# One fused attention, gated-MLP and channel-mix kernel: the five engine queues put in an order that a table writes out

## The chip, the cores and the metric

The program runs on one core of a Trainium2 chip. A core has five engines with a queue of instructions each: PE (matrix products), DVE (vector), ACT (scalar functions), POOL (a second, slower vector engine) and SP, which here issues every DMA transfer. Each queue runs in its own order; where an instruction needs another engine's result, it waits on a semaphore, and everything behind it in its queue waits with it. The metric is the device time of one launch in microseconds (us), the median of several executions.

## The reference

Three layers run one after the other on float32 data, with B=4 batches, 8 heads, 576 positions and 64 channels a head.

```python
# attention, causal, with a cumulative bias
cum = np.cumsum(np.maximum(s, 0.0), axis=-1)
bias = -(cum[:, :, :, None] - cum[:, :, None, :])
scores = np.where(causal, -1e9, q @ k.T / sqrt(D) + np.minimum(bias, 0.0))
attn = np.exp(scores - max);  attn = attn / (sum + 1e-9);  out = attn @ v
# gated MLP: 512 -> 1024, mixing over positions with w_sg, 512 -> 512
h = gelu(x @ w_in);  u, v = h[..., :512], h[..., 512:]
v_n = (v - mu) / np.sqrt(var + 1e-06) * g_ln
x = x + (u * (einsum('ts,bsd->btd', w_sg, v_n) + b_sg)) @ w_out
# channel mix
xk = mu_k * x + (1 - mu_k) * x_prev;  xr = mu_r * x + (1 - mu_r) * x_prev
y = sigmoid(xr @ w_r) * (np.maximum(xk @ w_k, 0) ** 2 @ w_v)
```

## The kernel before

Every float32 product is made of products of a "hi" part (rounded) and a "lo" part (what the rounding left), three for one. So each operand is split: a cast makes the hi part, and `split_lo` (L70) subtracts it from the original to make the lo part.

**Attention** works by pairs of heads, 16 pairs in all, `attn_pair` (L220). For head number n, a 128-row tile `kq` holds k above q. A cast (L243) puts q's hi part in the lower rows of `QB`, and another (L244) k's hi part in the upper rows of `ka`. Two DMAs (L245, L246) copy these to the other halves, of `qa` and `ka`. Two subtractions by `split_lo` (so their line in the profile is L71) make the lo parts: the lower half of `qa` from `kq` and `QB`, and the lower half of `KB` from `kq` and `ka`. From head 4 on, POOL makes both and the cast to `QB`. Two small DMAs (L234, L235) put rows of the cumulative sum into `QB` and `KB`. The tile numbers count heads: `qa14` is the first head of pair 7. Scores are then two matmuls, L267 (with `ka`, `qa`) and L268 (with `KB`, `QB`), into PSUM tile `sc`; DVE masks them and takes the maximum (L294), ACT takes the exponential (L299), PE transposes (L314, L317, L325, into `tp`, `tq`), ACT or DVE copies the result to SBUF (`pt1`, `pt2`, L319 to L327), and PE multiplies by v (L354, `pv`). In `sc6_1_3`, 6 is the pair, 1 the second head, 3 the block of rows.

`QB`, `KB`, `qa`, `ka` and `kq` have two buffers each, so head 16's `kq` is loaded (L229) into the buffer that head 14's `qa` subtraction read last.

**The gated MLP** of batch b (`moe1`, L399) runs beside the attention of batch b+1: products `v`, `u`, `sg`, `o` all go through `gemm3` (L386). For the first batch its weights `wc` are also made there: `first_wc` (L184) loads half a block of 256 columns as 64-bit words (`wr`, L197), `convert` (L76) turns them to float32 with two ACT operations (L78, L83) and two on DVE (L84, L86) on a tile `wy`, a cast on ACT (L89) and a subtraction on DVE (L71) make `wcs`, and L200 stores them to DRAM. Layer norm of `v` is POOL's (L442 to L444) with the split of the normed `vn` (ACT cast L446, POOL subtraction L71). The approximate gelu is two ACT operations and two on DVE (L552 to L555).

**The channel mix** follows alone: `k` and `r` products (L386), then 7 products in the place of 8 for `k*k @ w_v` (L829).

**What sets the order.** A scheduler that knows a cost for each instruction puts every engine's instructions in order when the program is built. Two things steer it: the sequence in which the code emits work (a generator `a_stream` for attention is advanced beside `moe1` by the rates `RATE` and `LEAD`), and `after(late, early)` (L539), which only forbids `late` to stand ahead of `early`, with no wait of its own.

Of the kernel before, what the change touches and what calls it, by code (L numbers as in the profile page):

```python
# [34 lines left out]
RATE = (1.1, 1, 1, 1)  # L35


@with_exitstack
def fused_kernel(ctx, tc, kqT, vL, s, w_in, g_ln, w_sgT, b_sg, w_out, mu_k, mu_r, w_k, w_v, w_r, out):
    nc = tc.nc  # L40

    const = ctx.enter_context(tc.tile_pool(name="const", bufs=1))
    dram = ctx.enter_context(tc.tile_pool(name="dram", bufs=1, space=bass.MemoryType.DRAM))
# [78 lines left out]
    with tc.high_priority():  # L122
# [7 lines left out]
        for i in range(NSET + 1):  # L130
            eng = nc.gpsimd if i else nc.vector
# [502 lines left out]
    turn, last = [0], [None]  # L634
# [196 lines left out]
    for p in range(TOK // PW):  # L831
# [8 lines left out]
        a = psum2.tile([P, 1 if last_p else 2, 512], F32, tag="ps", name=f"psa_{p}", bufs=4)  # L840
        b, c = (psum2.tile([P, 2, 512], F32, tag="ps", name=f"ps{n}_{p}", bufs=4) for n in "bc")
        if last_p:
            a = (a[:, 0], psum2.tile([P, 1, 512], F32, tag="ps", name=f"psa2_{p}", bufs=4)[:, 0])
# [10 lines left out]
        def block(h, c, ps, r):  # L854

            t = vb.tile([P, 2, HW], F32, tag="t", name=f"t{p}_{h}{c}", bufs=4)
            t0 = p * PW + c * HW
            g = vb.tile([P, 2, HW], F32, tag="gt", name=f"gt{p}_{h}{c}", bufs=3)
            nc.sync.dma_start(out=g, in_=gdram[h][:, :, t0:t0 + HW])
            for i, x in banks(ps):  # L860
                if r is None:
                    nc.vector.scalar_tensor_tensor(out=t[:, i], in0=x, scalar=1.0 / WS, in1=g[:, i], op0=ALU.mult, op1=ALU.mult)
                else:
                    nc.vector.scalar_tensor_tensor(out=t[:, i], in0=x, scalar=1.0 / WS, in1=r[:, i], op0=ALU.mult, op1=ALU.add)
            if r is not None:
                nc.vector.tensor_tensor(out=t, in0=t, in1=g, op=ALU.mult)
            for i in range(2):
                nc.sync.dma_start(out=out[2 * h + i].rearrange("p b s -> p (b s)")[:, t0:t0 + HW], in_=t[:, i])
# [13 lines left out]
        product(a, xs, 4)  # L882
        block(1, 0, a, None)


# [45 lines left out]
```

## Time and profile before

| | |
|---|---|
| median of 3 executions | 648.99 us (648.87 to 653.36) |
| profiled execution | 650.32 us, its span 648.3 us |
| busy: PE / DVE / ACT / POOL | 617.2 / 479.7 / 414.6 / 220.5 us |
| granted clock of PE over the span | 0.997 of full |

The span is the time from the first to the last record of the profiled execution; its own time has 2.0 us more around it. Busy time is the sum over an engine's instructions. In a timeline each row is one instruction or a run of equal ones, with its start and its duration; a bracket gives how long the engine had been idle and what ended the idle time. The granted clock is 1.00 at the full rate of 2.4 GHz and 0.50 at 1.2 GHz.

### The profile page before, as it was taken

The numbers are of one execution on the slowest core, as the hardware profiler recorded it, in microseconds if no ns is written. First come the engines' busy times: TensorE is split into PE (matmuls) and PEld (weight loads), VectorE is DVE, ScalarE is ACT, GpSimd is POOL, SyncE is SP. The second block draws the span as 40 slices with busy tenths as digits, with TensorE's granted clock in tenths as the row PEclk, the third lists the DMA queues.
The fourth block names the chain that finished last, engine by engine and source line by source line (L and its number), as shares of the span: only waits on it lengthen the run. The fifth ranks groups of instructions, "written<-read, shape, count | busy, mean of one in ns | idle before, by whom it ended". The sixth has DMA issues, their size and how long they took to land.

```text
span 648.3 us, 11284 instructions
## 1 busy us (share of the span) xinstructions
PE 617.2 (95%) x3768; PEld 535.7 (83%) x3768; DVE 479.7 (74%) x986; ACT 414.6 (64%) x937; POOL 220.5 (34%) x218
## 2 busy tenths in 40 slices
PE   1879999999999999999999999999999999999997
PEld 1657777878778987888897999888888888999997
DVE  7999788995659844579632878388897869586964
ACT  3889889974658844668641864278766878553530
POOL 7366649688528676267261200000000000000000
PEclk9899999999999999999999999999999999999999
DMA  7776664465553653735314974576764793646543
GB/s 212 186 236 209 162 201 113 154 189 139 182 189 92 176 138 89 234 95 132 110 24 144 316 261 126 144 243 209 244 211 181 233 344 138 198 162 205 208 146 122
DMA packets 68521, 115.08 MB, mean 178 GB/s; under 512 B 19744, under 2 KB 32688, under 8 KB 68464
## 3 DMA queue, kind: packets, MB, share of 16 engines
q1 hardware_dynamic: 68464, 114.37, 56.6%
q8 instruction: 30, 0.49, 0.3%
q14 instruction: 27, 0.22, 0.1%
HBM read 75.63 MB, written 29.20 MB: 162 GB/s over the span
## 4 chain that ended last, share of the span: by engine, by line
PE 80%; DMA 7%; DVE 6%; ACT 4%; issue 2%; SPq 1%; DVEq 0%; ACTq 0%
PE k L386 15%; PE sg L386 8%; PE psa L829 8%; PE r L386 8%; PE o L386 7%; PE v L386 6%; PE u L386 6%; PE pv L354 5%; PE psb L829 4%; PE tp L317 4%; PE sc L267 3%; PE sc L268 3%; PE psc L829 2%; ACT st L299 1%; DMA wsr<-in_w_sgT_dram 1%
## 5 line engine op out<-in xcount | busy, mean ns | idle before, releaser
L386 PE MATMUL k<-x,wk 128*128 128x512 f32 (+1 forms) x480 | 98.9, 368 | 0.0
L386 PEld LDWEIGHTS k<-x,wk 128*128 128x128 f32 x480 | 83.6, 189 | 14.9
L299 ACT ACTIVATE st<-st,mx 128x384 f32<-128x384 f32 (+4 forms) x128 | 75.1, 588 | 17.5 <-DVE mx L294 16.1
L267 PE MATMUL sc<-ka,qa 128*128 128x512 f32 (+3 forms) x180 | 61.1, 356 | 20.2 <-DMA ka<-ka 15.1
L294 DVE CUSTOM_DVE_ANT_0 st<-sc,mask 128x512 f32<-128x512 f32 (+3 forms) x128 | 62.5, 501 | 14.2 <-PE sc L268 11.1
L386 PE MATMUL sg<-wsg,vn 128*128 128x288 f32 x448 | 63.6, 297 | 0.3 <-DVE ga L485 0.3
L386 PEld LDWEIGHTS sg<-wsg,vn 128*128 128x128 f32 x448 | 60.4, 188 | 1.4 <-DVE ga L485 0.6
L268 PE MATMUL sc<-KB,QB 128*128 128x512 f32 (+3 forms) x180 | 56.3, 333 | 0.0
L267 PEld LDWEIGHTS sc<-ka,qa 128*128 128x128 f32 x180 | 33.1, 186 | 26.8 <-issue 18.7
L317 PE MATMUL tp<-ident,st 128*128 128x128 f32 x316 | 50.8, 279 | 0.6 <-ACT st L299 0.3
L354 PE MATMUL pv<-pt,vf 128*64 128x320 f32 (+4 forms) x448 | 50.6, 364 | 0.0
L386 PE MATMUL r<-x,wr 128*128 128x512 f32 (+1 forms) x240 | 49.5, 368 | 0.0
L386 PE MATMUL v<-wv,xs 128*128 128x512 f32 x192 | 48.4, 397 | 0.0
L386 PEld LDWEIGHTS r<-x,wr 128*128 128x128 f32 x240 | 41.9, 189 | 7.5
L648 ACT ACTIVATE yx<-yt,mu 128x64 f32<-128x64 f32 (+4 forms) x64 | 30.4, 529 | 26.5 <-DMA yt<-ydram 25.4
L354 PEld LDWEIGHTS pv<-pt,vf 128*64 128x64 f32 x448 | 29.2, 136 | 20.9 <-issue 3.2
L71 POOL TENSOR_TENSOR KB<-kq,ka 64x576 fp32r<-64x576 f32 x29 | 44.8, 1545 | 4.0 <-ACT ka L244 1.6
L71 POOL TENSOR_TENSOR qa<-kq,QB 64x576 fp32r<-64x576 f32 x29 | 44.7, 1541 | 2.1
L317 PEld LDWEIGHTS tp<-ident,st 128*128 128x128 f32 x316 | 38.5, 143 | 6.1 <-ACT st L299 1.0
L651 DVE SCALAR_TENSOR_TENSOR yx<-yt,mu,yx 128x64 f32<-128x64 f32 (+4 forms) x64 | 30.9, 515 | 14.3 <-ACT yx L648 14.3
L386 PE MATMUL u<-xs,wc 128*128 128x288 f32 x288 | 41.4, 297 | 0.0
L386 PEld LDWEIGHTS v<-wv,xs 128*128 128x128 f32 x192 | 35.0, 188 | 7.2 <-issue 0.2
(198 smaller groups left out, 1407.4 us busy)
## 6 DMA issues: line engine op xcount, KB each, us to landing
wc<-wscr SPq DMA_DIRECT2D x24, 512.0 KB
kq<-in_kqT_dram SPq DMA_DIRECT2D x32, 288.0 KB
kr<-kdram SPq DMA_DIRECT2D x12, 768.0 KB
kdram<-k SPq DMA_DIRECT2D x16, 512.0 KB
yt<-ydram SPq DMA_DIRECT2D x24, 257.0 KB
vf<-in_vL_dram SPq DMA_DIRECT2D x16, 320.0 KB
gt<-gdram SPq DMA_DIRECT2D x12, 384.0 KB
out_dram<-t SPq DMA_DIRECT2D x24, 192.0 KB
```

The lines of the kernel that those rows point to most:

```text
L71: eng.tensor_tensor(out=lo, in0=x, in1=f32(hi), op=ALU.subtract)
L267: nc.tensor.matmul(sc[:m, :c1 - c0], qa[:, q], ka[:, c0:c1], start=True, stop=False)
L268: nc.tensor.matmul(sc[:m, :c1 - c0], qb[:, q], kb[:, c0:c1], start=False, stop=True)
L294: mi = nc.vector.tensor_tensor_reduce(out=st[:, c0:c1], in0=sc[:, :n], in1=mk, op0=ALU.add, op1=ALU.min, scale=-SCALE, scalar=mx[:, 0:1] i ...
L299: e = nc.scalar.activation(st[:, :w], st[:, :w], AF.Exp, bias=mx[:, last:last + 1], scale=-1.0, accum_out=sm[:, i + 5 * (hh == 1):i + 5 * ...
L317: nc.tensor.transpose(tp[:, c:c + P], st[:, j * P:(j + 1) * P], ident)
L354: both.append(nc.tensor.matmul(acc[64 * a:64 * a + 64, o:n], vf[:, a, kk], pt, start=(kk == 0), stop=(kk == nk - 1)))
L386: nc.tensor.matmul(acc, a, w_, start=(i == 0), stop=(i == n - 1))
L648: i = nc.scalar.mul(t[:, s0:s1], yt[:, s0 + d:s1 + d], mu[:, r, 1, k:k + 1])
L651: nc.vector.scalar_tensor_tensor(out=t[:, s0:s1], in0=yt[:, s0 + d + 1:s1 + d + 1], scalar=mu[:, r, 0, k:k + 1], in1=t[:, s0:s1], op0=ALU. ...
L829: nc.tensor.matmul(to[:, :HW], l, r, start=(start and i == 0), stop=(i == len(mms) - 1), skip_group_check=True)
```

## The change

A wrapper around the five engines notes each emitted instruction in a list, in the order of emission. A table `ORDER` holds, for each engine, a sequence of numbers into that list, and at the end of the kernel each instruction is chained by `after` to the one that stands ahead of it in the table, so the table alone sets each queue. The instructions and their number are the same. (All rows now carry the line of the wrapper, L189.)

```diff
+ORDER = {
+    "tensor": (
...
+    "gpsimd": (
+        "0-1 6 3-4 8-9 2 7 5 10 12-14 16 11 17 15 18 20-21 19 23 22 24-28 30 29 31-34 36 35 37-38 51-54 56 55 "
...
+class Line:
...
+    def __getattr__(self, name):
...
+        def emit(*a, **k):
+            r = f(*a, **k)
+            if hasattr(r, "ins") and hasattr(r.ins, "name"):
+                self.emitted.append(r)
+            return r
+        return emit
...
+    def written(self):
+
+        for n, text in ORDER.items():
+            emitted, last = getattr(self, n).emitted, None
+            for run in text.split():
+                a, _, b = run.partition("-")
+                for i in range(int(a), int(b or a) + 1):
+                    if last is not None:
+                        yield emitted[i], last
+                    last = emitted[i]
...
-    nc = tc.nc
+    nc = Lines(tc.nc)
...
+    for late, early in nc.written():
+        after(late, early)
```

The resulting queues differ from those before in some 47 short moves of one or a few instructions: 12 places on PE, about 17 on ACT, 6 on DVE, 3 on POOL and 5 pairs on SP, nearly all beside attention (about 10 to 400 us). The places that follow lie near 113 to 125 us, where the first batch's MLP runs beside pairs 6 and 7.

POOL before. `qa14` and `KB1` belong to heads 14 and 15, `rstd0`, `v0`, `vn1_0` to the layer norm:

```order
L444 TENSOR_SCALAR v0_1012<-v0_1012,mv0_1014,rstd0_1015 128x512
L71 TENSOR_TENSOR vn1_0_1017<-v0_1012,vn0_0_1016 128x512
L71 TENSOR_TENSOR qa14_1808<-kq14_1804,QB0_89 64x576
L443 TENSOR_TENSOR rstd0_1015<-rstd0_1015,mhalf_71 128x1
L243 CAST QB1_90<-kq15_1819 64x576
L71 TENSOR_TENSOR KB1_92<-kq15_1819,ka15_1824 64x576
L71 TENSOR_TENSOR vn1_0_1017<-v0_1012,vn0_0_1016 128x512
L442 TENSOR_SCALAR rstd0_1015<-mv0_1014 64x1
L444 TENSOR_SCALAR v0_1012<-v0_1012,mv0_1014,rstd0_1015 128x512
L71 TENSOR_TENSOR qa15_1823<-kq15_1819,QB1_90 64x576
```

POOL after:

```order
L189 TENSOR_SCALAR v0_1012<-v0_1012,mv0_1014,rstd0_1015 128x512
L189 TENSOR_TENSOR vn1_0_1017<-v0_1012,vn0_0_1016 128x512
L189 TENSOR_TENSOR rstd0_1015<-rstd0_1015,mhalf_71 128x1
L189 CAST QB1_90<-kq15_1819 64x576
L189 TENSOR_TENSOR KB1_92<-kq15_1819,ka15_1824 64x576
L189 TENSOR_TENSOR vn1_0_1017<-v0_1012,vn0_0_1016 128x512
L189 TENSOR_SCALAR rstd0_1015<-mv0_1014 64x1
L189 TENSOR_SCALAR v0_1012<-v0_1012,mv0_1014,rstd0_1015 128x512
L189 TENSOR_TENSOR qa14_1808<-kq14_1804,QB0_89 64x576
L189 TENSOR_TENSOR qa15_1823<-kq15_1819,QB1_90 64x576
```

The subtraction that makes `qa14` moves behind six instructions, to just ahead of that of `qa15`.

SP before, the DMA queue at the same place:

```order
L254 DMA vf7_1816<-in_vL_dram 128x640
L197 DMA wr4_0_1508<-in_w_out_dram 128x2x256
L234 DMA QB1_90<-cumd_62 2x576
L235 DMA KB1_92<-cumd_62 2x576
L246 DMA ka15_1824<-ka15_1824 64x576
L229 DMA kq16_2092<-in_kqT_dram 128x576
L197 DMA wr4_1_1517<-in_w_out_dram 128x2x256
```

SP after:

```order
L189 DMA vf7_1816<-in_vL_dram 128x640
L189 DMA QB1_90<-cumd_62 2x576
L189 DMA wr4_0_1508<-in_w_out_dram 128x2x256
L189 DMA KB1_92<-cumd_62 2x576
L189 DMA ka15_1824<-ka15_1824 64x576
L189 DMA kq16_2092<-in_kqT_dram 128x576
L189 DMA wr4_1_1517<-in_w_out_dram 128x2x256
```

The row of `QB1`, which overwrites what the scores of head 13 read, now goes ahead of the load of weights `wr4_0`. The load of `kq16`, into the buffer that the `qa14` subtraction reads, stands where it did, ahead of `wr4_1`.

DVE before, where the converted weights `wy4_1` meet the copies of pair 6:

```order
L71 TENSOR_TENSOR wcs4_1507<-wy4_0_1509,wcs4_1507 128x256
L321 COPY pt2_6_1475<-tp6_1_3_1675 128x4x128
L294 ISA st7_0_3_1880,mx7_0_3_1881<-sc7_0_3_0_1882,mask_88 128x512
L294 ISA mx7_0_3_1881 128x1
L84 SCALAR_TENSOR_TENSOR wy4_1_1518<-wr4_1_1517,wy4_1_1518 128x256
L327 COPY pt2_6_1475<-tq6_1595 128x2x64
L555 SCALAR_TENSOR_TENSOR u0_2_1527<-u0_2_1527,u0_2_0_1528 128x288
```

DVE after:

```order
L189 TENSOR_TENSOR wcs4_1507<-wy4_0_1509,wcs4_1507 128x256
L189 SCALAR_TENSOR_TENSOR wy4_1_1518<-wr4_1_1517,wy4_1_1518 128x256
L189 COPY pt2_6_1475<-tp6_1_3_1675 128x4x128
L189 ISA st7_0_3_1880,mx7_0_3_1881<-sc7_0_3_0_1882,mask_88 128x512
L189 ISA mx7_0_3_1881 128x1
L189 COPY pt2_6_1475<-tq6_1595 128x2x64
L189 SCALAR_TENSOR_TENSOR u0_2_1527<-u0_2_1527,u0_2_0_1528 128x288
```

The first DVE step of `wy4_1` moves ahead of the copy of `tp6_1_3` and of the masking of `sc7_0_3`; it stood ahead of the copy of `tq6` already.

The other moves of this stretch are of the same kind. On ACT, the copy of `tp6_2_4` to `pt2_6` goes behind six instructions, and one exponential goes ahead of L83 of `wy4_0`; on PE, the transposes of `tp6_1_1` go behind the 12 matmuls of `u0_2_0`. Earlier, near 13 us, POOL's cast to `QB_f` goes ahead of the subtraction that makes `qa1`. Moves after 176 us are single exchanges of neighbours.

## Rows read from the trace of the kernel before

**Rows 1.** Table by stage: stretch, length, busy us by engine, granted clock, DMA share, GB/s.

```profile
118.72:131.73 13.01, 11.19 (x78) 9.42 (x77) 12.20 (x36) 13.01 (x39) 8.40 (x8) 1.00 0.50 175
131.73:146.05 14.32, 14.00 (x106) 11.74 (x106) 14.19 (x25) 10.23 (x28) 11.52 (x9) 1.00 0.57 165
...
176.00:648.30 472.30, 468.86 (x2773) 415.35 (x2771) 334.92 (x632) 276.60 (x580) 103.96 (x112) 1.00 0.56 177
```

**Rows 2.** Timeline of POOL, 113 to 121 us: start, duration, engine, line, operation, tiles.

```profile
113.09 1.50 POOL L71 TENSOR_TENSOR qa<-kq,QB 64x576 fp32r<-64x576 f32 x1
114.67 0.63 POOL L443 TENSOR_TENSOR rstd<-rstd,mhalf 128x1 f32<-128x1 f32 x1
115.36 0.70 POOL L243 CAST QB<-kq 64x576 fp32r<-64x576 f32 x1
116.14 1.43 POOL L71 TENSOR_TENSOR KB<-kq,ka 64x576 fp32r<-64x576 f32 x1
117.65 1.36 POOL L71 TENSOR_TENSOR vn<-v,vn 128x512 fp32r<-128x512 f32 x1
118.98 0.40 POOL L442 TENSOR_SCALAR rstd<-mv 64x1 f32<-64x1 f32 x1
119.37 2.09 POOL L444 TENSOR_SCALAR v<-v,mv,rstd 128x512 f32<-128x512 f32 x1
```

**Rows 3.** Timeline of PE, 113 to 128 us: in brackets the idle time before.

```profile
113.40 0.39 PE L268 MATMUL sc<-KB,QB 128*128 128x512 f32 x1
...
118.72 0.22 PE L267 MATMUL sc<-ka,qa 128*128 128x128 f32 x1
...
121.72 1.87 PE L386 MATMUL u<-xs,wcs 128*128 128x288 f32 x12 [0.32 <-DVE u L555]
...
125.06 3.44 PE L386 MATMUL u<-xs,wcs 128*128 128x288 f32 x24
```

**Rows 4.** Timeline of SP's queue: issue time, duration of the issue, what is moved.

```profile
113.33 0.39 SPq L197 DMA_DIRECT2D wr<-in_w_out_dram  x1
...
115.78 0.53 SPq L229 DMA_DIRECT2D kq<-in_kqT_dram  x1
119.32 0.39 SPq L197 DMA_DIRECT2D wr<-in_w_out_dram  x1
...
123.29 0.38 SPq L197 DMA_DIRECT2D wr<-in_w_out_dram  x1
```

**Rows 5.** Timeline of ACT, 117 to 126 us.

```profile
117.31 0.44 ACT L78 ACTIVATE wy<-wr 128x256 f32<-128x256 f32 x1 [1.49 <-DMA wr<-in_w_out_dram]
...
126.00 0.43 ACT L78 ACTIVATE wy<-wr 128x256 f32<-128x256 f32 x1
```

**Rows 6.** Timeline of DVE, 123 to 125 us.

```profile
123.18 0.68 DVE L321 COPY pt<-tp 128x512 f32<-128x512 f32 x1
123.78 0.67 DVE L294 CUSTOM_DVE_ANT_0 st<-sc,mask 128x512 f32<-128x512 f32 x1
...
124.39 0.41 DVE L84 SCALAR_TENSOR_TENSOR wy<-wr,wy 128x256 uint32<-128x256 uint32 x1
124.73 0.28 DVE L327 COPY pt<-tq 128x128 f32<-128x128 f32 x1
```

**Rows 7.** Timeline of POOL near 13 us.

```profile
12.80 1.75 POOL L71 TENSOR_TENSOR qa<-kq,QB 64x576 fp32r<-64x576 f32 x1
14.50 1.49 POOL L243 CAST QB_f<-kq 64x576 fp32r<-64x576 f32 x1
```

**Rows 8.** Timeline of PE near 26 us.

```profile
26.27 0.30 PE L267 MATMUL sc<-ka_f,qa_f 128*128 128x128 f32 x1 [1.61 <-DMA ka_f<-ka_f]
```

**Rows 9.** Table by stage of three early stretches.

```profile
27.70:30.60 2.90, 2.90 (x13) 2.50 (x12) 2.90 (x8) 2.90 (x10) 2.47 (x2) 0.50 0.47 106
43.90:46.00 2.10, 0.00 (x0) 0.02 (x1) 2.10 (x7) 2.10 (x8) 1.97 (x2) 1.00 1.02 290
46.00:49.00 3.00, 2.99 (x24) 2.34 (x25) 2.90 (x9) 2.73 (x7) 0.63 (x2) 1.00 1.00 362
```

More of the change, by code (lines that the diff above doesn't have):

```diff
@@ L35, with __init__, __getattr__ @@
 RATE = (1.1, 1, 1, 1)
+ORDER = {
+    "tensor": (
[40 rows of a table added]
+    ),
+    "vector": (
[31 rows of a table added]
+    ),
+    "scalar": (
[30 rows of a table added]
+    ),
+    "gpsimd": (
[7 rows of a table added]
+    ),
+    "sync": (
[18 rows of a table added]
+    ),
+}
+class Line:
+    def __init__(self, eng):
+        self.eng, self.emitted = eng, []
+    def __getattr__(self, name):
+        f = getattr(self.eng, name)
+        if not callable(f):
+            return f
+        def emit(*a, **k):
[4 more added lines that the diff above has]
+        return emit
+class Lines:
+    def __init__(self, nc):
+        self.nc = nc
+        for n in ORDER:
+            setattr(self, n, Line(getattr(nc, n)))
+    def __getattr__(self, name):
+        return getattr(self.nc, name)
+    def written(self):
[7 more added lines that the diff above has]
+                    last = emitted[i]
 @with_exitstack
 def fused_kernel(ctx, tc, kqT, vL, s, w_in, g_ln, w_sgT, b_sg, w_out, mu_k, mu_r, w_k, w_v, w_r, out):
-    nc = tc.nc
+    nc = Lines(tc.nc)
     const = ctx.enter_context(tc.tile_pool(name="const", bufs=1))
```

125 rows, old and new, of the table ORDER are left out of this document.

## The prediction, made before the changed kernel was run

> **What bounds the kernel now.** I read the table by stage first. PE is the busiest engine, and from 176 us on it is busy 468.86 of 472.30 us [rows 1]: whatever delays PE in the first part reaches the end, since nothing after it has idle time to give back, and a gain there would reach the end too. Near most of the moves PE has little left to win. From 118.72 to 131.73 it is busy 11.19 of 13.01 us, from 131.73 to 146.05 it is busy 14.00 of 14.32 [rows 1]: its idle time there is 1.82 + 0.32 = 2.14 us, and that is all that moves in this place can bring. In the same first stretch DVE works 12.20 and ACT 13.01 of the 13.01 us, so neither has slack to absorb a late input. Then come the timelines of the engines around that place. POOL runs its row of work from 113.09 to 121.46 without a pause [rows 2], PE asks for `qa14` at 118.72 without any idle time ahead of it [rows 3], and SP's queue issues loads in strict order [rows 4].
>
> **The change, part by part.** The same instructions run, so no work is added or removed, and all that counts is when each input is ready.
>
> *The subtraction for `qa14` on POOL.* It ran from 113.09 for 1.50 us, long before PE's `sc7_0_0` at 118.72 [rows 2, 3]. Now six instructions go ahead of it: the small L443, the cast to `QB1`, `KB1`, `vn`, L442 and L444. L443 (0.63 us) can start at about 113.05, but the cast writes `QB1`, which PE reads until `sc6_1_3` ends at 113.40 + 0.39 = 113.79 [rows 3]. I let it start at 113.85. From the start of the cast to the end of L444 it took 119.37 + 2.09 - 115.36 = 6.10 us [rows 2], with POOL never waiting, and the inputs (ACT's casts `ka15` and `vn0`) come no later than they did, since ACT has lost the copy of `tp6_2_4` ahead of them. So L444 ends near 119.95, and `qa14` near 119.95 + 0.08 + 1.50 = 121.5. PE's transposes and matmuls ahead of `sc7_0_0` are the same set in another order, so PE arrives at 118.72 as before and waits until 121.5: **2.8 us of new idle time on PE**. Nothing else fills it, because PE's queue is in order and everything of the `u` products that is ready stands behind.
>
> *What is queued behind POOL's late read.* The load of `kq16` overwrites the buffer that this subtraction reads. It was issued at 115.78, and now cannot be before 121.5. Behind it on SP stands the load `wr4_1`, issued at 119.32 [rows 4], now near 121.55 + 0.53 = 122.1. The time from issue to ACT's first use has two rows: 113.33 to 117.31 is 3.98 us, and 123.29 to 126.00 is 2.71 us [rows 4, 5]. ACT's L78 and L83 then take about 0.9 us (starts 0.33 apart, the second of about 0.5), and DVE's L84, which now stands ahead of the copy of `tp6_1_3`, 0.41; then DVE still has the copy, the masking and the copy of `tq6`, 123.18 to 124.39 and 0.28 us [rows 6]. PE's `u0_3_0`, which began at 125.06 right behind that last copy [rows 3], is so bound to 122.1 + (2.71 to 3.98) + 0.9 + 0.41 + 1.21 + 0.28, which is 127.6 to 128.9: 2.5 to 3.8 us late. By PE's own work alone it would come earlier: 118.72 to 125.06 are 6.34 us, with at most the 1.82 us of idle time of the stretch in them [rows 1], so `u0_3_0` would be 1.0 to 2.8 us late. Two chains therefore meet here, and the later one decides. I take 2.8 us, which is the stall itself and lies near the lower end of the later chain, because `wr4_1` has only the load of `kq16` right ahead of it, and the row of 2.71 us is then the nearer one.
>
> *`QB1` ahead of `wr4_0` on SP.* The row of `QB1` can't be issued before 113.79, and `wr4_0` went at 113.33 [rows 4]; it becomes about 1.1 us later. ACT had already waited 1.49 us for it [rows 5], so this wait grows by as much, to some 2.6 us, and `u0_1_1` and the copy `pt2_6`, both behind it on ACT, come later. PE needs that copy for the next transposes after `sc7`, at about 122.4 in the new schedule: they are hidden behind the wait for `qa14`. If that wait were not there, this would cost up to 1.1 us. Cost now 0.
>
> *DVE's and ACT's moves there* are counted in the chain above. The transposes of `tp6_1_1` behind `u0_2_0` move PE's work within a stretch without idle time: 0.
>
> *Early moves.* The cast to `QB_f` goes ahead of the subtraction for `qa1` near 13 us. The cast took 1.49 us and the subtraction 1.75 [rows 7], so one gains at most 1.75 and the other loses at most 1.49; what waits later is PE for the DMA of `ka_f`, 1.61 us at 26.27 [rows 8]. As that wait ends with a DMA and not with POOL, I take 0, with bounds of -1.6 (the whole wait gone) and +1.5. The middle of this is far likelier than its ends, and I carry 0.7 either way in the range.
>
> *The remaining moves*, from about 20 to 105 us and the single exchanges after 176 us, pass instructions whose inputs were there earlier or whose users still wait for something else: 0 each, and after 176 us PE has 3.44 us of idle time in all [rows 1], which bounds any gain there.
>
> **Sum.** Against the profiled execution: 650.32 + 2.8 + 0 = 653.1. The median of the runs shown is 1.33 us below that execution, so the prediction for the median is 648.99 + 2.8 = **651.8 us**.
>
> **A rule against this.** After idle stretches this chip's trace shows PE at half its clock once: the granted clock is 0.50 from 27.70 to 30.60. It stays 1.00 after the stretch from 43.90 to 46.00, in which PE did nothing [rows 9]. The Trainium skill ("TensorE: Matmul & The Clock Gate", section "What's actually happening") says that the throttled clock is the default and activity releases it; by that rule the new idle time could bring the low level back, while the second row here speaks against it for a single stall after dense work. I keep it as a rival.
>
> **The rivals.**
> - *Absorbed.* PE's idle time of 2.14 us after 118.72 was spent on inputs of DVE and ACT. If those are ready by the time that PE is 2.8 us late, it is eaten up, and 2.8 - 2.14 = 0.7 stays: 649.7. For it: DVE and ACT don't wait for `qa14` until its scores are masked. Against it: both are nearly full in this stretch [rows 1], and DVE's queue itself is held up by `wr4_1`.
> - *Clock.* The stall takes the clock to 0.50 for a stretch as long as the 2.90 us seen [rows 9]. Work done there takes twice its time, so up to 1.45 us more: +4.25, or 653.2. For it the low stretch seen after sparse work; against it the full clock after 43.90 to 46.00.
> - *Faster.* POOL reaches `qa14` in time, and the moves of `tp6_1_1`, `wy4_1` and `pt2_6` close the gaps of 118 to 146 us: 2.14 less, or 646.9. The point that decides is 117.2: POOL must begin `qa14` by then, so the instructions from the cast on would have to take 3.3 in place of 6.1 us. The rows give POOL five instructions that sum to 5.98 us of busy time without their gaps [rows 2]; only a contention with DVE that vanished could shorten them, and not by half.
> - *Nothing changes*, if the scheduler had let other bounds decide: 649.0. The order printed shows that the queues did change.
>
> **How the numbers follow.** Forecast 0.60, absorbed 0.15, clock 0.14, faster 0.08, no change 0.03. The forecast alone has 2.5 to 3.8 us and 0.7 either way, so 650.8 to 653.5. The range goes on to the absorbed case with its 0.7 (649.0) and a little below, and to the clock with its own (653.9): 648.7 to 654.0, which leaves out the faster case and the ends of the early bound, together under 0.2. One per cent, 6.5 us, is about what a measurement of this kernel can tell from no change; no case gets there by itself, and the unknown ends of the sum give 0.04 for slower and 0.02 for faster.
>
> **What would show it.** Right: in the changed trace PE idles about 2.8 us ahead of `sc7_0_0`, ended by POOL's `qa`, L71; POOL has `qa14` directly ahead of `qa15`; the load of `kq16` is issued near 121.5; `u0_3_0` starts 2 to 4 us later than 125.06; and PE's busy time from there on is the same. Wrong: `sc7_0_0` without idle time ahead, or idle time that the stretch up to 146 us has given back, or a clock under 1.00 behind the stall, or PE's waits at 26 and 46 us changed by over 0.7 us.

## The result, and the profile after

Timed side by side, the changed kernel takes 655.23 us (median of 22 executions, 651.07 to 659.2), the kernel before 650.31 us (22 executions). The ratio is 1.0071, with a 95% interval of 1.0050 to 1.0091: **slower by 4.6 us, 3.3 to 5.9**. The forecast was slower by 2.8, to 651.8; the range to 654.0 does not hold the result. The profiled execution took 655.32 us, its span is 653.2 us and the clock 0.992.

PE's timeline after, with the idle time in brackets; every row now has the line of the wrapper:

```profile
114.68 3.34 PE L189 MATMUL u<-xs,wcs 128*128 128x288 f32 x24
118.68 1.87 PE L189 MATMUL u<-xs,wcs 128*128 128x288 f32 x12 [0.66 <-DVE u L189]
...
123.56 0.33 PE L189 MATMUL sc<-ka,qa 128*128 128x128 f32 x1 [2.68 <-POOL qa L189]
...
129.98 3.45 PE L189 MATMUL u<-xs,wcs 128*128 128x288 f32 x24 [0.20 <-DVE pt L189]
...
136.42 0.38 PE L189 MATMUL sc<-ka,qa 128*128 128x256 f32 x1 [1.00 <-DVE mx L189]
```

The stall that was forecast is there: `sc7_0_0` at 123.56 waits 2.68 us, and POOL's `qa` ends the wait (in [rows 3] it started without idle time). The next two rows are `u0_3_0`, with a short wait for DVE's copy, and the scores `sc7_1_1`. For a common ruler I measure the *stretch* from the start of `u0_1_0` (113.63 before, 114.68 here) to the start of `sc7_1_1` (131.34 before, 136.42 here) on PE. It was 17.71 us and is 21.74: **+4.03 us in this one place**. From the start of `sc7_1_1` to the end of the span there are 516.96 us before and 516.78 after, so what the stretch loses is still there at the end. The long last part has 3.53 us of idle time, 3.44 before [rows 1]. The table by stage after (length, busy us by engine, clock, DMA, GB/s):

```profile
68.72:80.00 11.28, 11.28 (x71) 8.15 (x71) 5.54 (x18) 7.85 (x22) 5.81 (x5) 0.85 0.42 127
114.68:123.56 8.88, 5.54 (x41) 5.06 (x39) 6.99 (x17) 6.97 (x19) 8.57 (x8) 1.00 0.21 67
123.56:129.98 6.42, 6.22 (x34) 5.67 (x34) 5.28 (x17) 4.12 (x13) 1.96 (x2) 0.73 0.75 236
129.98:136.42 6.44, 5.44 (x40) 4.92 (x40) 5.47 (x14) 6.29 (x17) 3.20 (x2) 1.00 0.52 175
...
181.00:653.20 472.20, 468.67 (x2771) 415.28 (x2770) 333.92 (x631) 275.93 (x580) 104.18 (x112) 1.00 0.55 177
```

The first row is a stretch earlier (from the scores `sc4_2_4` to `sc5_0_0`) and the third the one behind the stall: in both the granted clock was at its low level for part of the time. POOL's row of work (start, duration) is this, to be read against [rows 2]:

```profile
114.48 0.74 POOL L189 TENSOR_TENSOR rstd<-rstd,mhalf 128x1 f32<-128x1 f32 x1
115.30 0.72 POOL L189 CAST QB<-kq 64x576 fp32r<-64x576 f32 x1
116.10 1.82 POOL L189 TENSOR_TENSOR KB<-kq,ka 64x576 fp32r<-64x576 f32 x1
118.00 1.34 POOL L189 TENSOR_TENSOR vn<-v,vn 128x512 fp32r<-128x512 f32 x1
119.31 0.39 POOL L189 TENSOR_SCALAR rstd<-mv 64x1 f32<-64x1 f32 x1
119.69 2.33 POOL L189 TENSOR_SCALAR v<-v,mv,rstd 128x512 f32<-128x512 f32 x1
122.11 2.78 POOL L189 TENSOR_TENSOR qa<-kq,QB 64x576 fp32r<-64x576 f32 x2
```

The last row is `qa14` and `qa15` together; `qa14` ended at 123.50. SP, ACT and DVE then show the chain behind it, in this order ([rows 4 to 6] before):

```profile
123.53 0.33 SPq L189 DMA_DIRECT2D kq<-in_kqT_dram  x1
123.96 0.39 SPq L189 DMA_DIRECT2D wr<-in_w_out_dram  x1
```

```profile
127.21 0.43 ACT L189 ACTIVATE wy<-wr 128x256 f32<-128x256 f32 x1 [1.00 <-DMA wr<-in_w_out_dram]
```

```profile
124.03 0.29 DVE L189 CUSTOM_DVE_ANT_0 st<-sc,mask 128x128 f32<-128x128 f32 x1 [2.36 <-PE sc L189]
...
128.09 0.42 DVE L189 SCALAR_TENSOR_TENSOR wy<-wr,wy 128x256 uint32<-128x256 uint32 x1 [0.67 <-ACT wy L189]
128.44 0.68 DVE L189 COPY pt<-tp 128x512 f32<-128x512 f32 x1
129.04 0.68 DVE L189 CUSTOM_DVE_ANT_0 st<-sc,mask 128x512 f32<-128x512 f32 x1
...
129.64 0.28 DVE L189 COPY pt<-tq 128x128 f32<-128x128 f32 x1
```

The load of `kq16` is issued as soon as `qa14` is read, `wr4_1` behind it; ACT waits 1.00 us for that load, then DVE's L84, the two copies and the masking run without a pause until 129.92, and PE's `u0_3_0` starts at 129.98. (The row of DVE at 124.03 is the masking of `sc7_0_0`.)

### The profile page after: what moved, and what is told of

Read it like the earlier page. It is cut to its first block, busy times and chain, and to the rows that moved or that the text cites. A ratio compares the mean times of both kernels' runs of the same rounds, so it can differ in the third digit from the quotient of the medians.

```text
span 653.2 us, 11286 instructions
## 1 busy us (share of the span) xinstructions
PE 621.6 (95%) x3768; PEld 539.4 (83%) x3768; DVE 476.9 (73%) x986; ACT 414.4 (63%) x937; POOL 221.5 (34%) x218
## 2 busy tenths in 40 slices
DMA packets 68521, 115.08 MB, mean 176 GB/s; under 512 B 19744, under 2 KB 32688, under 8 KB 68464
## 4 chain that ended last, share of the span: by engine, by line
PE 78%; DVE 6%; ACT 5%; DMA 4%; issue 3%; POOL 2%; SPq 1%; DVEq 0%; ACTq 0%; POOLq 0%
PE k L189 15%; PE sg L189 8%; PE psa L189 8%; PE r L189 8%; PE o L189 7%; PE v L189 6%; PE sc L189 6%; PE u L189 6%; PE pv L189 5%; PE psb L189 4%; PE tp L189 4%; PE psc L189 2%; DVE st L189 2%; ACT st L189 1%; DMA kq<-in_kqT_dram 1%
## 5 line engine op out<-in xcount | busy, mean ns | idle before, releaser
L189 PE MATMUL k<-x,wk 128*128 128x512 f32 (+1 forms) x480 | 98.9, 368 | 0.0
L189 PEld LDWEIGHTS k<-x,wk 128*128 128x128 f32 x480 | 83.6, 189 | 14.9
L189 ACT ACTIVATE st<-st,mx 128x384 f32<-128x384 f32 (+4 forms) x128 | 75.0, 588 | 18.4 <-DVE mx L189 16.0
L189 PE MATMUL sc<-ka,qa 128*128 128x512 f32 (+3 forms) x180 | 62.3, 362 | 20.5 <-DMA ka<-ka 12.1
L189 DVE CUSTOM_DVE_ANT_0 st<-sc,mask 128x512 f32<-128x512 f32 (+3 forms) x128 | 62.4, 501 | 21.4 <-PE sc L189 20.9
L189 PE MATMUL sg<-wsg,vn 128*128 128x288 f32 x448 | 63.6, 297 | 0.2 <-DVE ga L189 0.2
L189 PEld LDWEIGHTS sg<-wsg,vn 128*128 128x128 f32 x448 | 60.4, 188 | 1.1 <-issue 0.3
L189 PE MATMUL tp<-ident,st 128*128 128x128 f32 x344 | 55.7, 280 | 2.1 <-ACT st L189 2.1
L189 PE MATMUL sc<-KB,QB 128*128 128x512 f32 (+3 forms) x180 | 57.2, 338 | 0.0
L189 PEld LDWEIGHTS sc<-ka,qa 128*128 128x128 f32 x180 | 33.8, 190 | 27.0 <-ACT ka L189 11.8
L189 PE MATMUL pv<-pt,vf 128*64 128x320 f32 (+4 forms) x448 | 52.1, 370 | 0.8 <-ACT pt L189 0.8
L189 ACT COPY pt<-tp 128x384 f32<-128x384 f32 (+1 forms) x88 | 43.5, 510 | 13.5 <-PE tp L189 12.7
L189 PE MATMUL r<-x,wr 128*128 128x512 f32 (+1 forms) x240 | 49.5, 368 | 0.0
L189 PEld LDWEIGHTS tp<-ident,st 128*128 128x128 f32 x344 | 42.1, 143 | 8.5 <-ACT st L189 2.9
L189 PEld LDWEIGHTS pv<-pt,vf 128*64 128x64 f32 x448 | 29.8, 138 | 22.6 <-issue 4.4
L189 PE MATMUL v<-wv,xs 128*128 128x512 f32 x192 | 48.4, 397 | 0.0
L189 PEld LDWEIGHTS r<-x,wr 128*128 128x128 f32 x240 | 41.9, 189 | 7.5
L189 ACT ACTIVATE yx<-yt,mu 128x64 f32<-128x64 f32 (+4 forms) x64 | 30.3, 529 | 27.2 <-DMA yt<-ydram 26.3
L189 POOL TENSOR_TENSOR KB<-kq,ka 64x576 fp32r<-64x576 f32 x29 | 45.2, 1557 | 6.6 <-ACT ka L189 4.4
L189 POOL TENSOR_TENSOR qa<-kq,QB 64x576 fp32r<-64x576 f32 x29 | 43.7, 1507 | 1.9
L189 PE MATMUL u<-xs,wc 128*128 128x288 f32 x288 | 41.3, 296 | 0.0
L189 PEld LDWEIGHTS v<-wv,xs 128*128 128x128 f32 x192 | 35.0, 188 | 7.2 <-issue 0.2
```

The source lines that it names most:

```text
L189: r = f(*a, **k)
```

## The experiments

In the three profiles with the order of before (before, 1 and 5) the stretch is 17.71 us each time, while the start of `u0_1_0` itself lies anywhere from 110.9 to 116.6 us in the thirteen profiles. So the stretch is the finer measure, though each is read from one profiled execution, and the ratio says whether the whole agrees. Rows of it stand with the experiments; all of it together:

| kernel | starts of `u0_1_0`, `sc7_1_1` | stretch | ratio to before (95% interval) |
|---|---|---|---|
| before | 113.63, 131.34 | 17.71 | 1 |
| changed | 114.68, 136.42 | 21.74 | 1.0071 (1.0050 to 1.0091) |
| 1 table of before | 116.02, 133.73 | 17.71 | 1.0004 (0.9985 to 1.0023) |
| 2 qa14 back | 113.97, 132.67 | 18.70 | 1.0021 (1.0000 to 1.0042) |
| 3 qa14 alone | 114.31, 136.08 | 21.77 | 1.0042 (1.0024 to 1.0060) |
| 4 stall filled | 115.08, 136.71 | 21.63 | 1.0069 (1.0041 to 1.0097) |
| 5 moves elsewhere | 116.64, 134.35 | 17.71 | 0.9996 (0.9969 to 1.0022) |
| 6 load free | 116.22, 136.45 | 20.23 | 1.0070 (1.0045 to 1.0095) |
| 7 load free, filled | 115.24, 135.46 | 20.22 | 1.0057 (1.0032 to 1.0083) |
| 8 qa14 three later | 114.19, 133.06 | 18.87 | 1.0011 (0.9987 to 1.0035) |
| 9 qa14, pt2 back | 110.85, 129.10 | 18.25 | 1.0018 (0.9999 to 1.0038) |
| 10 qa14, wr4 back | 114.93, 133.14 | 18.21 | 0.9999 (0.9975 to 1.0024) |
| 11 qa14 four later | 114.44, 133.68 | 19.24 | one execution, 652.4 us |

**1. The table alone.**

```diff
 ORDER = {
-    (the changed order)
+    (the order that the scheduler gave before, as numbers)
```

> The order of before, written out by the same table and chained, with none of the moves. If the moves are the cause: ratio to before 1.000 +- 0.002. If the chaining itself costs something: up to the 1.007 of the change. It also shows how often the granted clock of an execution of the old order lies below 0.997, which says how much of the change's clock of 0.992 is ordinary spread.

The chaining costs nothing that can be measured. Over its 12 executions the mean clock is 0.992, over the 34 of before beside it 0.993: the 0.997 of the profiled execution of before was one of its better ones, and 0.992 after is no sign of the change.

**2 and 3. The one move on POOL, taken back and made alone.** (73 is `qa14`'s subtraction, 59 L444.)

```diff
 "gpsimd" of 2, from the changed kernel
-... 49 46 58 75 77 50 61 59 73 76 ...
+... 49 46 73 58 75 77 50 61 59 76 ...
 "gpsimd" of 3, from before
-... 49 46 73 58 75 77 50 61 59 76 ...
+... 49 46 58 75 77 50 61 59 73 76 ...
```

> The changed kernel with the one POOL subtraction of qa14 back at its old place; all other moves stay. Theory A (the qa14 stall of 2.7 us and the low clock behind it, 1.4 us, are the loss): ratio to before 1.000 to 1.002, no idle time ahead of sc7_0_0 and no low clock near 125 us. Theory B (the other moves carry a good part, through the low clock near 70 us and the wait for u at 118.7): 1.003 to 1.005, with the low clock at 70 us still there.

> Before with the one move of the qa14 subtraction on POOL and nothing else. Theory A: +2.7 us of stall and +1.4 us of clock less up to 2.1 us of idle time eaten up after it, so +2.5 to +4.5 us, ratio 1.004 to 1.007. Theory B: +0.7 to +2 us, ratio 1.001 to 1.003.

PE in 2 and then in 3:

```profile
113.97 4.92 PE L189 MATMUL u<-xs,wcs 128*128 128x288 f32 x36
...
118.97 0.31 PE L189 MATMUL sc<-ka,qa 128*128 128x128 f32 x1
...
121.36 0.66 PE L189 MATMUL tp<-ident,st 128*128 128x128 f32 x4 [0.86 <-ACT pt L189]
...
132.67 0.39 PE L189 MATMUL sc<-ka,qa 128*128 128x256 f32 x1 [0.74 <-DVE mx L189]
```

```profile
114.31 3.34 PE L188 MATMUL u<-xs,wcs 128*128 128x288 f32 x24
...
122.52 0.47 PE L188 MATMUL sc<-ka,qa 128*128 128x128 f32 x1 [2.75 <-POOL qa L188]
...
136.08 0.39 PE L188 MATMUL sc<-ka,qa 128*128 128x256 f32 x1 [0.81 <-DVE mx L188]
```

Alone, the move makes a stretch as long as the whole change (21.77, +4.06). Over the whole program it costs 2.7 us (1.6 to 3.9), so the 4.06 of its one profile is a little above what its executions show. And the path behind the stall is another one than in the changed kernel. The table by stage from `sc7_0_0` to `u0_3_0` in 3, and DVE's row in it:

```profile
122.52:129.86 7.34, 7.34 (x35) 7.05 (x35) 5.04 (x17) 3.74 (x12) 1.94 (x2) 0.57 0.65 203
```

```profile
129.48 0.29 DVE L188 COPY pt<-tq 128x128 f32<-128x128 f32 x1 [1.57 <-PE tq L188]
```

The granted clock is 0.57 on the mean, PE works through all of the 7.34 us without a wait, and DVE's copy of `tq6` waits 1.57 us for PE. So in 3 the low clock holds up `u0_3_0`, and not the load. What 3 would take at the full clock was not run.

Taken back (2), the stall is gone and no low clock falls there, and 0.99 us stay, with a new wait of 0.86 us for an ACT copy at 121.36. So the other moves here do cost, but only when the wait for `qa14` doesn't hide them: 0.99 and 4.06 don't add up to more than 4.03.

**4. The stall filled with work.** (549 is the last transpose of `tp6_1_1`, 642 `sc7_0_0`.)

```diff
+                if (pr, hh, i) == (7, 0, 0):
+                    for _ in range(22):
+                        fill.append(tc.nc.tensor.transpose(sc[:, 0:P], ident, ident))
...
+    for d, e in zip(fill, [pe[549]] + fill):
+        after(d, e)
+    after(pe[642], fill[-1])
```

> The changed kernel with 22 transposes of the identity put into PE's wait ahead of sc7_0_0 (into the bank that sc7_0_0 then overwrites); the wait for qa14 stays. If the low clock behind the stall comes from PE's idle time there: granted clock 1.00 from 124 to 130 us, and 1.2 to 1.6 us less than the changed kernel, ratio to before about 1.005. If the clock falls for another reason, or costs nothing: low clock still near 125 us, ratio about 1.007.

```profile
120.74 2.56 PE L467 MATMUL sc<-ident 128*128 128x128 f32 x22
...
128.97 0.52 PE L189 MATMUL tp<-ident,st 128*128 128x128 f32 x3 [0.98 <-DVE pt L189]
129.69 3.45 PE L189 MATMUL u<-xs,wcs 128*128 128x288 f32 x24 [0.20 <-DVE pt L189]
...
136.71 0.39 PE L189 MATMUL sc<-ka,qa 128*128 128x256 f32 x1 [1.60 <-DVE mx L189]
```

```profile
123.31:129.69 6.38, 5.14 (x35) 4.23 (x35) 5.28 (x17) 4.32 (x14) 1.96 (x2) 1.00 0.78 225
```

SP, ACT and DVE in 4, at the next load of weights behind `wr4_1`:

```profile
127.24 0.38 SPq L189 DMA_DIRECT2D wr<-in_w_out_dram  x1
```

```profile
131.36 0.43 ACT L189 ACTIVATE wy<-wr 128x256 f32<-128x256 f32 x1 [0.72 <-DMA wr<-in_w_out_dram]
```

```profile
132.25 0.42 DVE L189 SCALAR_TENSOR_TENSOR wy<-wr,wy 128x256 uint32<-128x256 uint32 x1 [1.56 <-ACT wy L189]
```

The clock stays at 1.00, as expected, and the gain does not come: 21.63 in place of 21.74. From `sc7_0_0` to `u0_3_0` it is 6.38 us, and 6.42 at the low clock of the changed kernel: PE does its work faster and then waits for DVE, 0.98 us at 128.97 where the changed kernel waited 0. The low clock was hidden behind something else. In this execution `sc7_0_0` and `u0_3_0` come 0.65 and 0.69 us earlier after `u0_1_0` than in the profile of the changed kernel (8.23 against 8.88, 14.61 against 15.30), since POOL ended `qa14` that much earlier. That is lost again ahead of `sc7_1_1`, where PE waits 1.60 us and not 1.00: ACT waits 0.72 us for the next load, and DVE 1.56 us for ACT.

**5. All moves outside this place.** (The changed table, with 8 moves on PE, 2 on DVE, 6 on ACT, 1 on POOL and 2 on SP between 105 and 131 us taken back.)

> All moves but those between 105 and 131 us, which stay as before: only the early moves (up to 100 us) and the late ones. Theory A (one place costs everything): ratio 1.000 +- 0.002, and the stretch from u0_1_0 to sc7_1_1 on PE as long as before, 17.71 us. Theory B (the early moves cost about 1 us, through the low clock near 70 us): 1.001 to 1.003, with that low clock in the trace.

```profile
116.64 3.34 PE L188 MATMUL u<-xs,wcs 128*128 128x288 f32 x24
...
134.35 0.39 PE L188 MATMUL sc<-ka,qa 128*128 128x256 f32 x1 [0.85 <-DVE mx L188]
```

0.9996 (2.0 us less to 1.4 more), and the same stretch of 17.71 us with the same last wait. The moves elsewhere cost and gain nothing that can be measured.

**6 and 7. The load behind `qa14`.** (166 is `kq16`, 127 `wr4_1`, 151 `qa15`'s copy.)

```diff
 "sync", from the changed kernel (7: with the 22 transposes of 4 as well)
-... 150 152 166 127 151 114 ...
+... 150 152 127 151 166 114 ...
```

> The changed kernel with one exchange on SP: the load of kq16, which must wait for the late qa14, goes behind wr4_1 and qa15 instead of ahead of them. If the queue behind kq16 sets u0_3_0 (late weights wy4_1, then DVE's copies): wr4_1 issued 2 to 3 us earlier, no wait of ACT for it, and the stretch from u0_1_0 to sc7_1_1 shorter than the 21.74 us of the change, 20.5 to 21. If PE's own work at the low clock is as long: 21.4 to 21.8, unchanged, although ACT's wait is gone.

> The same exchange, and PE's wait for qa14 filled with 22 transposes of the identity. If the low clock and the load chain lay on top of one another behind the stall, each hidden by the other: the stretch from u0_1_0 to sc7_1_1 falls to 20.2 to 20.8 us (PE's work of 5.4 to 5.6 us from sc7_0_0 to u0_3_0 in place of 6.4). If something else bounds it: 21.4 to 21.8.

SP and PE in 7:

```profile
121.47 0.38 SPq L189 DMA_DIRECT2D wr<-in_w_out_dram  x1
...
123.44 0.35 SPq L189 DMA_DIRECT2D kq<-in_kqT_dram  x1
```

```profile
129.13 3.45 PE L189 MATMUL u<-xs,wcs 128*128 128x288 f32 x24 [0.20 <-DVE pt L189]
...
135.46 0.39 PE L189 MATMUL sc<-ka,qa 128*128 128x256 f32 x1 [0.91 <-DVE mx L189]
```

```profile
123.47:129.13 5.66, 5.15 (x35) 4.23 (x35) 5.18 (x17) 4.35 (x14) 1.95 (x2) 1.00 0.58 198
```

The weights are loaded 2 us ahead of `kq16`, and from `sc7_0_0` to `u0_3_0` PE now needs 5.66 us where 4 needed 6.38. Between 4 and 7, both at the full clock, the load chain is worth 21.63 - 20.22 = **1.41 us**. Of this 0.72 us arise by `u0_3_0`. The other 0.69 come behind it, by the next load: it is issued 12.16 us after `u0_1_0` in 4 and 12.15 in 7, and ACT uses it 4.12 us later in 4 (131.36) and 2.72 in 7 (130.11). In 6 the low clock happened not to fall behind the stall, so it repeats 7 (20.23, a little under the 20.5 to 21 expected) and can't show the low clock without the load chain; in the changed order that case was not seen. The ratios of 6 and 7 can't tell 1.4 us, and the profiled execution of 6 lost 2.4 us just after the stretch (16.78 us in place of 14.38 from `sc7_1_1` to `sg0_2_0`), which 7 with the same order did not. Whether the exchange pays over the whole program stays open.

**8 and 11. Half the distance.**

```diff
 "gpsimd", from before
-... 49 46 73 58 75 77 50 61 59 76 ...
+... 49 46 58 75 77 73 50 61 59 76 ...     (8)
+... 49 46 58 75 77 50 73 61 59 76 ...     (11)
```

> Before with qa14's subtraction on POOL moved behind three instructions (L443, the cast to QB1, KB1) and not six. POOL then ends it near 117.6 to 118 on the clock of before, ahead of PE's need at 118.7: no idle time ahead of sc7_0_0, the stretch from u0_1_0 to sc7_1_1 17.7 to 18.0 us, ratio 1.000. If any delay of qa14 costs, by the load of kq16 behind it: 18.5 us or more.

> Before with qa14's subtraction behind four instructions of POOL (three gave a stretch of 18.87 us, six 21.77). It then ends about 1.4 us later than behind three, near 5.8 us after u0_1_0 starts, against PE's need at 5.1. If its end against PE's need decides: idle time of about 0.7 us ahead of sc7_0_0 and a stretch between the two, 19 to 20 us. If a late qa14 costs by contention of POOL and DVE for the most part: no order by distance, below 18.9 or above 20.5.

In 8, `qa14` is ready in time (it ends at 118.60, and `sc7_0_0` starts at 119.49, 0.2 us later after `u0_1_0` than before), PE shows no wait for it, and still 1.16 us are lost. DVE and POOL show why. DVE in 8, POOL in 8, and DVE before:

```profile
115.35 1.97 DVE L188 TENSOR_TENSOR xT<-xT,rb 128x576 f32<-128x576 f32 x1
...
117.67 0.54 DVE L188 CUSTOM_DVE_ANT_0 st<-sc,mask 128x384 f32<-128x384 f32 x1
```

```profile
115.20 1.50 POOL L188 TENSOR_TENSOR KB<-kq,ka 64x576 fp32r<-64x576 f32 x1
116.76 1.84 POOL L188 TENSOR_TENSOR qa<-kq,QB 64x576 fp32r<-64x576 f32 x1
```

```profile
114.79 0.75 DVE L370 TENSOR_TENSOR xT<-xT,rb 128x576 f32<-128x576 f32 x1
...
115.89 0.54 DVE L294 CUSTOM_DVE_ANT_0 st<-sc,mask 128x384 f32<-128x384 f32 x1
```

DVE's product of two SBUF operands (`xT`) takes 1.97 us in place of 0.75. It ends at 117.32, which is 0.62 us after POOL's `KB1` ended at 116.70, so it looks as if it had waited for POOL and then run (0.62 us is a little less than its 0.75); POOL's next one, `qa14`, started in that time and took 1.84 in place of 1.50. Everything behind on DVE is 1.2 us late, and PE meets that as a wait of 1.11 us for `sc7_0_3`. The Trainium skill ("SBUF — State Buffer", section "SBUF: two separate sides") says that a DVE operation with two SBUF inputs and a POOL operation that reads SBUF contend for a shared pair of ports; the one that starts first has it as an exclusive lock for its whole instruction, and the other one fully blocks. These rows agree: `KB1` starts at 115.20 and `xT` at 115.35. In 11 a wait for POOL appears (0.38 us, where I expected 0.7) and the stretch lies between 8 and 3, as expected if the distance decides. But `xT` takes 1.98 us in 11 and in 3 too, so those 1.2 us on DVE come with the new place of `KB1` in all three and not with the distance, and `sc7_0_3` starts 8.14 us after `u0_1_0` in 8 and 11 alike (7.04 before). What 11 loses beyond 8, 0.37 us, comes behind that; the runs do not say how much of it is the distance.

```profile
120.28 0.33 PE L188 MATMUL sc<-ka,qa 128*128 128x128 f32 x1 [0.38 <-POOL qa L188]
...
133.68 0.39 PE L188 MATMUL sc<-ka,qa 128*128 128x256 f32 x1 [1.18 <-DVE mx L188]
```

**9 and 10. What is left when qa14 is back.** (193 is the copy of `tp6_2_4`, 126 `wr4_0`, 149 the row of `QB1`.)

```diff
 from the kernel of experiment 2
 "scalar" (9)
-... 162 220 130 195 170 181 197 182 172 193 171 ...
+... 162 193 220 130 195 170 181 197 182 172 171 ...
 "sync" (10)
-... 147 149 126 150 ...
+... 147 126 149 150 ...
```

> The changed kernel with qa14's subtraction and, on ACT, the copy of tp6_2_4 to pt2_6 back at their old places. With qa14 back alone, PE waited 0.86 us for a copy by ACT and the stretch from u0_1_0 to sc7_1_1 took 18.70 us, 0.99 more than before. If ACT's late copy is the cause: 17.7 to 18.0 us and no such wait. If the late load of wr4_0 is the cause (it holds up ACT, and the copies behind it): still 18.4 to 18.9.

> The changed kernel with qa14's subtraction back and, on SP, the load wr4_0 ahead of the row of QB1 again; ACT's copy stays late. The other way round: if the late load is the cause of the 0.99 us, the stretch from u0_1_0 to sc7_1_1 takes 17.7 to 18.0 us; if ACT's late copy is, 18.4 to 18.9.

```profile
117.78 0.66 PE L189 MATMUL tp<-ident,st 128*128 128x128 f32 x4 [0.55 <-ACT pt L189]
```

```profile
121.49 0.66 PE L189 MATMUL tp<-ident,st 128*128 128x128 f32 x4 [0.17 <-ACT pt L189]
```

Neither expectation holds: each takes away about half (0.45 and 0.49 of the 0.99 us), and PE's wait for ACT goes from 0.86 to 0.55 and 0.17. The late copy and the first use of the late load both stand in ACT's queue, and their shares sum to nearly the 0.99; both taken back together was not run.

## Why the prediction was wrong

**The place and the cause were right.** POOL's `qa14` behind six instructions, 2.8 us of idle time on PE forecast and 2.68 measured; alone it makes a stretch as long as the whole change (3), there by the low clock in place of the load. The moves elsewhere were put at 0, and nothing of them can be measured (5).

**The step that failed is the price of the chain behind the stall.** The prediction had two chains at `u0_3_0`, PE's own with 1.0 to 2.8 us and the load's with 2.5 to 3.8, said that the later one decides, and then took 2.8, the stall itself, near the lower end. Measured from the start of `u0_1_0`, `u0_3_0` came 129.98 - 114.68 - (125.06 - 113.63) = 3.87 us late, and the stretch lost 4.03. The chain ran as it was drawn; two of its terms were too small in the profile:
- POOL ended `qa14` 123.50 - 114.68 = 8.82 us after `u0_1_0`, where the forecast has 121.53 - 113.63 = 7.90. The cast to `QB1` began 0.62 us after `u0_1_0` and not 0.22, `KB1` took 1.82 us and L444 2.33, against 1.43 and 2.09 in [rows 2]. Only about 0.3 of these 0.92 us is the change: in 4, 6 and 7, with the same order on POOL and DVE, `KB1` took 1.83 too, but L444 2.09, and `qa14` ended 8.16 to 8.18 us after `u0_1_0`. The rest belongs to this execution. That `KB1` is longer because other work of DVE runs beside it now is likely after 8, but no run shows it for this order. That durations on POOL stay as they were was assumed and not said as a bound.
- The load took 3.25 us from issue to use (3.18 in 4), not the 2.71 of the row that I called the nearer one.

The forecast also ended the chain at `u0_3_0`. In 4, where POOL ended `qa14` only 0.28 us later than forecast and `u0_3_0` came 3.18 us late, the next load made up the difference and the stretch still lost 3.92.

So in place of 2.8 there are the 2.5 us that the stall leaves without the load chain (7: 20.22 against 17.71), the load chain's 1.41 (4 against 7) and some 0.1: the 4.03 us.

**The base and the range.** The upper end of the load's chain, 3.8 us, was close to the 3.87 and 4.03 measured. But it was set on 648.99, the median of three executions; 22 executions of the same kernel have 650.31. The forecast is 3.4 us short of the result: 1.3 by this base, 1.2 by the stretch (4.03 in place of 2.8), and 0.9 that the stretch does not show and that lie within the interval of the difference. On the base of 650.31 the same range would have ended at 655.3. It had no term for the base, although the three executions already spread from 648.87 to 653.36. The prediction also took one per cent, 6.5 us, as about what a measurement of this kernel can tell from no change; the interval here is 2.6 us wide.

**The clock rival was half right.** The clock did fall behind the stall in the profiled execution (0.73 on the mean from 123.56 to 129.98), which I gave 0.14 and named as a sign of being wrong. It fell behind PE's waits of 2.68 us there and 2.75 us in 3, and not behind 2.40 us in 6. In the changed kernel it cost nothing, because the load chain was as long (4). Where that is not so, the clock does cost: in 3 it holds up `u0_3_0`, and the +4.06 us there are close to this rival's 4.25, though how much of them is the clock was not run. Elsewhere it costs too: from `sc4_2_4` to `sc5_0_0` the changed kernel's profile has 11.28 us at a mean clock of 0.85, and before 9.71 at 1.00, so 1.57 us. That fall belongs to the one execution: it is not in the profiles of 2 and 4 to 7, which have the same order there. The same stretch before:

```profile
68.87:78.58 9.71, 9.71 (x70) 7.49 (x71) 6.67 (x22) 8.87 (x24) 5.83 (x6) 1.00 0.50 147
```

**QB1 ahead of `wr4_0`** was put at 0 while the stall hides it and at up to 1.1 us without: no sign of it in the changed kernel (21.74, and 21.77 in 3 without it), and 0.99 without the stall, shared with ACT's late copy (2, 9, 10). That held, except that the copy has about half of it.

**The absorbed case fell** for only one of the reasons given against it. DVE did have room: it stood still for 2.36 us until `sc7_0_0` came and for 0.67 until ACT's `wy4_1` did. It could not use it, since its queue waited for PE's late scores and for the late weights, so PE's inputs came no earlier. PE's wait ahead of `sc7_1_1` was 0.86 before and 1.00 after.

## What to carry to other kernels

When an instruction is moved back, don't stop at the engine that waits for it: ask which buffer it frees, which transfer waits for that, and what stands behind that transfer in its queue; if two chains meet, price the later one by its own terms, and follow it past the first place where they meet. An operation that moves to another time can take longer or shorter there, so its old duration is no bound: on POOL `KB1` went from 1.43 to 1.83 us, and L442 from 0.40 to 0.22 (4, 6 and 7). And two delays that overlap can't be found by taking away one: filling the stall alone showed nothing, and it took the load's exchange as well to see what the load was worth. Two kernels can also lose the same time by different paths, as 3 and the change do: an equal number does not show an equal cause.

## What the runs showed of the hardware

- Most of the spread of the executions (several microseconds for one kernel) arises ahead of 115 us: the stretch of 17.71 us repeats to 0.01 us in three profiles (before, 1 and 5), while its start lies between 113.6 and 116.6 us in them, and from `sc7_1_1` to the end it is 516.7 to 517.0 us in ten of the thirteen profiles.
- The mean granted clock of an execution says little of its time: over 77 executions of the kernel before (timed beside the experiments), those below 0.990 have a mean of 650.9 us (11), those at 0.995 and above 650.5 us (35).
- A product of two SBUF operands on DVE (0.75 us) took 1.97 us beside POOL's subtraction in 8 and 1.98 in 3 and 11, and POOL's own took up to 1.84 in place of 1.50 us.
